# Two tokens per partition for the first four chunks of a retention layer that feeds a gated FFN

## The chip, the cores and the metric

The kernel runs on one core of a Trainium2 chip. A core has TensorE (PE; its weight loads are shown apart as PEld), VectorE (DVE), ScalarE (ACT), GpSimd (POOL) and SyncE (SP), which run their own instruction streams and wait for each other by semaphores. Matmuls read SBUF and write PSUM; DVE and ACT read PSUM; transfers between main memory and SBUF are issued by SP ("hardware" queue), ACT or POOL ("software" queue, which can also convert float32 to bfloat16 on the way). The metric is the device time of one execution in microseconds, the median over several.

## What is computed

Queries, keys and values have shape (4 batches, 8 heads, 768 tokens, 64), all float32. Each head keeps a 64 x 64 state that decays by a factor gamma per token; the result, heads side by side, is a matrix x of 3072 tokens by 512, and goes through a gated FFN of width 1536:

```python
gamma = 1.0 - 2.0 ** (-5.0 - np.arange(H, dtype=np.float32))
for t in range(S):
    state = gamma * state + k[t]^T v[t]
    y[t] = scale * q[t] @ state
gate = 1.0 / (1.0 + np.exp(-(x @ w_gate)))
val = x @ w_val
out = (gate * val) @ w_out
```

## The kernel before

Tokens are cut into chunks of 128 (six to a batch, 24 in all, numbered g) and FFN tiles of 512 tokens (four chunks, six tiles, numbered t). Decay is put into tables: v is scaled by gamma^-s (`scale_v`, L167, table tabv), so that within a batch the state is a plain running sum, and the attention output is scaled by gamma^t (`y_out`, L240, table taby), which also moves it from PSUM to xT, the FFN's input, tokens along the free axis.

For a chunk, q and k are loaded as bfloat16 with tokens on partitions. PE transposes them (four 128 x 128 transposes each; a transpose is a matmul with the identity), ACT copies them to SBUF (qkT). `scores` (L172) makes the 128 x 128 products of keys and queries for eight heads: a head has 64 channels, so a pair of heads takes the upper and the lower half of the array's rows. `masks` (L180) lets DVE multiply them by a causal mask. `inter` (L206) adds q times the state of earlier chunks, which ACT has copied into the block-diagonal tiles zbd (`state_out`, L199); `intra` (L233) adds masked scores times v; `state_early` (L204) adds k^T v to the state in PSUM. Intra and state take half of the array's columns per head.

Two orders matter. The loop from L428 on runs FFN tile after FFN tile (`up`, L278: 4 + 4 matmuls for gate and value of one FFN block n1 of 128 columns, sigmoid on ACT, product on DVE; `down`, L310), with the attention steps of later chunks put between its groups by the table `plan`. Before it, L348 to L410 are a written-out beginning: chunks 0 to 2 go one after another, then `up` of blocks 0 to 3 for the first 384 tokens with chunk 3 in between, and `up_columns` (L292) for the last 128 tokens of these blocks. `keep_on` (L325) issues matmuls of the identity whose result nobody reads. Each engine executes in program order: the schedule is by hand, and only waits are inserted.

The loads are issued in this order. SP: k, q and v of chunk 0 as float32 (kf, qf on L89 to L92, converted on DVE and ACT on L356 and L357; vf). POOL: chunk 1, chunk 2, the first 256 columns of the gate and value weights (`load_gate_val`, L78), chunk 3, the second 256 columns, then the rest, `load_out` (L84) and chunks 4 to 7; two `scale_v` and two extensions of taby stand between them. PSUM has one bank for the state (pool pz) and seven (pool pf, tag ff) that everything else takes in turn, each waiting until the bank's last reader is done.

Of the kernel before, what the change touches and what calls it, by code (L numbers as in the profile page):

```python
# [9 lines left out]
F32 = mybir.dt.float32  # L10
BF16 = mybir.dt.bfloat16
I32 = mybir.dt.int32
AX = mybir.ActivationFunctionType
ALU = mybir.AluOpType
# [3 lines left out]
def kernel(  # L18
# [10 lines left out]
    nc = tc.nc  # L29
# [3 lines left out]
    C = 128  # L33
# [7 lines left out]
    ctx.enter_context(tc.manual_schedule())  # L41
    const = ctx.enter_context(tc.tile_pool(name="const", bufs=1))
    wpool = ctx.enter_context(tc.tile_pool(name="wpool", bufs=1))
    ld = ctx.enter_context(tc.tile_pool(name="ld", bufs=12))
    at = ctx.enter_context(tc.tile_pool(name="at", bufs=2))
    ffn = ctx.enter_context(tc.tile_pool(name="ffn", bufs=3))
    pz = ctx.enter_context(tc.tile_pool(name="pz", bufs=1, space=bass.MemoryType.PSUM))
# [8 lines left out]
    def src(x, g):  # L56
        b, c = divmod(g, NCH)
        return x[b, :, c * C:(c + 1) * C, :].rearrange("h s d -> s h d")

    def load_v(g, eng):  # L60
        vf[g] = ld.tile([C, H, D], F32, tag="vf", name="vf", bufs=8)
        eng.dma_start(out=vf[g], in_=src(v, g))  # L62

    def load_kq(g):
        kn[g] = ld.tile([C, H, D], BF16, tag="kn", name="kn")
# [3 lines left out]

    def load_chunk(g):  # L70
        load_kq(g)
        load_v(g, nc.gpsimd)

    wg = wpool.tile([128, KT, D_FF], BF16, name="wg")
    wv = wpool.tile([128, KT, D_FF], BF16, name="wv")
# [2 lines left out]
    def load_gate_val(s):  # L78
        cols = slice(s * 256, (s + 1) * 256)
        for dst, w in ((wg, moe_w_gate), (wv, moe_w_val)):  # L80
            nc.gpsimd.dma_start(out=dst[:, :, cols],  # L81
                                in_=w.rearrange("(kk p) n -> p kk n", p=128)[:, :, cols])

    def load_out(s):  # L84
# [1 line left out]
                            in_=moe_w_out.rearrange("(n p) d -> p n d", p=128)[:, s * 3:(s + 1) * 3, :])  # L86


    kf = const.tile([C, H, D], F32, name="kf")  # L89
    qf = const.tile([C, H, D], F32, name="qf")  # L90
    nc.sync.dma_start(out=kf, in_=src(k, 0))
    nc.sync.dma_start(out=qf, in_=src(q, 0))  # L92
    nc.scalar.preload_act_table(AX.Exp)
    load_v(0, nc.sync)
    tokv = const.tile([128, NCH], I32, name="tokv")
    nc.gpsimd.iota(tokv, pattern=[[C, NCH]], base=0, channel_multiplier=1)
    ident = const.tile([128, 128], BF16, name="ident")
    make_identity(nc, ident)
    toky = const.tile([128, 384], I32, name="toky")
    nc.gpsimd.iota(toky, pattern=[[1, 384]], base=0, channel_multiplier=0)  # L100
    load_chunk(1)
    causal = const.tile([128, 128], F32, name="causal")
    nc.gpsimd.memset(causal, 1.0)
    nc.gpsimd.affine_select(causal, causal, pattern=[[1, 128]], base=0, channel_multiplier=-1,
                            compare_op=ALU.is_ge, fill=0.0)
    load_chunk(2)

    tabv = const.tile([128, NCH, H], F32, name="tabv")
    for h in range(H):
        nc.scalar.activation(tabv[:, :, h], tokv, AX.Exp, scale=-lg[h])  # L110
    lgp = const.tile([128, NP], F32, name="lgp")
    lsc = const.tile([128, 1], F32, name="lsc")
    nc.vector.memset(lsc, math.log(scale))
# [6 lines left out]
    zbd = [const.tile([128, NP, C], BF16, name=f"zbd{i}") for i in range(4)]  # L120
    for t in zbd:
        nc.vector.memset(t, 0.0)
    taby = const.tile([128, NP, S], F32, name="taby")

    def make_taby(cols):
        for p in range(NP):
            nc.scalar.activation(taby[:, p, cols], toky[:, cols], AX.Exp, scale=lgp[:, p:p + 1], bias=lsc)

    def extend_taby(lo, hi):
        nc.gpsimd.tensor_tensor(taby[:, :, lo:hi], taby[:, :, lo - 384:hi - 384],  # L130
                                gup.unsqueeze(2).to_broadcast([128, NP, hi - lo]), op=ALU.mult)

    causal4 = causal.unsqueeze(1).to_broadcast([128, NP, 128])


# [1 line left out]
    zz, za = {}, {}  # L137

    def bank(shape, dt=F32):
        return pf.tile(shape, dt, tag="ff", name="ff", padded_shape=[128, 2 * NP, C] if dt == BF16 else None)  # L140

    def pair(t, p):
        return t[:, 2 * p:2 * p + 2, :].rearrange("s h d -> s (h d)")

    def transposes(g):
# [3 lines left out]
                nc.tensor.transpose(tp[:, i * NP + p, :], pair(x, p), ident)  # L149
        qkT[g] = at.tile([128, 2 * NP, C], BF16, tag="qkT", name="qkT", bufs=6)  # L150
        nc.scalar.activation(qkT[g], tp, AX.Copy)  # L151

    def transposes_early(g):
        qkT[g] = at.tile([128, 2 * NP, C], BF16, tag="qkT", name="qkT", bufs=6)
        for i, x in enumerate((kn[g], qn[g])):
            tp = bank([128, NP, C], BF16)
            for p in range(NP):
                nc.tensor.transpose(tp[:, p, :], pair(x, p), ident)
            nc.scalar.activation(qkT[g][:, i * NP:(i + 1) * NP], tp, AX.Copy)

    def xbar(g):
        qkT[g] = ld.tile([128, 2 * NP, C], BF16, tag="qkX", name="qkX", bufs=8)
# [4 lines left out]
    def scale_v(g, eng):  # L167
        vs[g] = ld.tile([C, H, D], BF16, tag="vs", name="vs", bufs=8)
        eng.tensor_tensor(vs[g], vf[g], tabv[:, g % NCH, :].unsqueeze(2).to_broadcast([C, H, D]),  # L169
                          op=ALU.mult)  # L170

    def scores(g):  # L172
        t = qkT[g]
        sc[g] = (bank([128, NP, C]), bank([128, NP, C]))
        for p in range(NP):
            for i in range(2):
                half = slice(i * D, (i + 1) * D)
                nc.tensor.matmul(sc[g][i][:, p, :], t[half, p, :], t[half, NP + p, :], start=True, stop=True)  # L178

    def masks(g):  # L180
        stA[g] = at.tile([128, NP, C], BF16, tag="stA", name="stA", bufs=4)
        stB[g] = at.tile([128, NP, C], BF16, tag="stB", name="stB", bufs=4)
        nc.vector.tensor_tensor(stA[g], sc[g][0], causal4, op=ALU.mult)  # L183
        nc.vector.tensor_tensor(stB[g], sc[g][1], causal4, op=ALU.mult)  # L184

    def inter(g):
        y[g] = bank([128, NP, C])
        if g % NCH > 0:
            for p in range(NP):
                nc.tensor.matmul(y[g][:, p, :], zbd[(g - 1) % 4][:, p, :], qkT[g][:, NP + p, :],  # L190
                                 start=(p == 0), stop=False, skip_group_check=True)
# [7 lines left out]
    def state_out(g, z):  # L199
        for i in range(2):  # L200
            half = slice(i * D, (i + 1) * D)
            nc.scalar.copy(zbd[g % 4][half, :, half], z[half])  # L202

    def state_early(g):  # L204
        if g == 0:
            zz[0] = pz.tile([128, 2, NP, D], F32, tag="z", name="z")  # L206
        z = zz[0][:, 0]
        for p in range(NP):
            for i in range(2):
                nc.tensor.matmul(z[i * D:(i + 1) * D, p, :], kn[g][:, 2 * p + i, :], vs[g][:, 2 * p + i, :],  # L210
                                 start=(g == 0 and p == 0), stop=True, skip_group_check=True)
        state_out(g, z)

    def new_za(g):
        za[g] = at.tile([128, NP, D], F32, tag="za", name="za", bufs=3)
        return za[g]
# [16 lines left out]
    def intra(g):  # L233
        first = g % NCH == 0
        for p in range(NP):
            for i, st in enumerate((stA[g], stB[g])):
                nc.tensor.matmul(y[g][i * D:(i + 1) * D, p, :], vs[g][:, 2 * p + i, :], st[:, p, :],  # L237
                                 start=(first and p == 0), stop=True, skip_group_check=True)

    def y_out(g):  # L240
        c = g % NCH
        if g % 4 == 0:
            xT[g // 4] = at.tile([128, NP, 512], BF16, tag="xT", name="xT")
        col = (g % 4) * C
        nc.vector.tensor_tensor(xT[g // 4][:, :, col:col + C], y[g], taby[:, :, c * C:(c + 1) * C], op=ALU.mult)  # L245

    def step_t(g):
        transposes(g)
# [76 lines left out]
    def keep_on(n):  # L325
        u = bank([128, 512])
        for _ in range(n):
            nc.tensor.matmul(u[:, :128], ident, ident, start=True, stop=True)  # L328
# [16 lines left out]
            first += width  # L345


    scale_v(0, nc.gpsimd)  # L348
    load_gate_val(0)
    scale_v(1, nc.gpsimd)  # L350
    load_chunk(3)
    load_gate_val(1)
    make_taby(slice(0, 256))
    kn[0] = ld.tile([C, H, D], BF16, tag="kn", name="kn")
    qn[0] = ld.tile([C, H, D], BF16, tag="qn", name="qn")
    nc.vector.tensor_copy(kn[0], kf)  # L356
    nc.scalar.copy(qn[0], qf)  # L357
    keep_on(30)
    transposes_early(0)
    make_taby(slice(256, 384))  # L360
    extend_taby(384, 512)
    for s in range(2, NFF // 2):
        load_gate_val(s)
    extend_taby(512, 768)
    for s in range(4):
        load_out(s)
    for g in range(4, 8):
        load_chunk(g)
    keep_on(8)
    scores(0)  # L370
    masks(0)
    keep_on(10)
    transposes_early(1)
    inter(0)
    state_early(0)
    intra(0)
    y_out(0)
    keep_on(8)
    scores(1)
    masks(1)  # L380
    keep_on(4)
    inter(1)
    transposes_early(2)
    state_early(1)
    nc.scalar.preload_act_table(AX.Sigmoid)
    intra(1)
    y_out(1)
    scale_v(2, nc.vector)
    keep_on(8)
    scores(2)  # L390
    masks(2)
    inter(2)
    keep_on(14)
    intra(2)
    state_early(2)
    y_out(2)
    up(0, 0, 0, 384)
    scale_v(3, nc.vector)
    transposes_early(3)
    up(0, 1, 0, 384)  # L400
    scores(3)
    masks(3)
    inter(3)
    state_early(3)
    up(0, 2, 0, 384)
    intra(3)
    y_out(3)
    nc.vector.tensor_copy(new_za(3), zz[0][:, 0])
    up(0, 3, 0, 384)
    up_columns(0, range(4), 384, 512)  # L410


    def ups(t):
# [88 lines left out]
```

## Time and profile before

| | us |
|---|---|
| median of 10 executions (233.75 to 237.55) | 234.37 |
| the profiled execution | 234.09 |
| its span, first to last instruction | 232.4 |
| first FFN matmul | 16.74 |
| first FFN matmul on all 512 tokens | 26.01 |
| PE busy | 223.1 (96%) |
| DVE, ACT, POOL busy | 110.8, 91.9, 92.4 |

The profile shows one execution. Its stage table gives busy time per engine; the list of instructions in order of time gives, for a group of like instructions, start, length (from the first's start to the last's end), engine, source line, operation, output and inputs, shape, count, and in brackets the idle time before and what ended it. A matmul's end is modelled, and matmuls are pipelined: those of 128 columns last 0.22 us each and follow each other much closer. `L285` is line 285 of the kernel before; line numbers of the changed kernel differ.

### The profile page before, as it was taken

The numbers are of one execution on the slowest core, as the hardware profiler recorded it, in microseconds if no ns is written. First come the engines' busy times: TensorE is split into PE (matmuls) and PEld (weight loads), VectorE is DVE, ScalarE is ACT, GpSimd is POOL, SyncE is SP. The second block draws the span as 40 slices with busy tenths as digits, with TensorE's granted clock in tenths as the row PEclk, the third lists the DMA queues.
The fourth block names the chain that finished last, engine by engine and source line by source line (L and its number), as shares of the span: only waits on it lengthen the run. The fifth ranks groups of instructions, "written<-read, shape, count | busy, mean of one in ns | idle before, by whom it ended". The sixth has DMA issues, their size and how long they took to land.

```text
span 232.4 us, 4448 instructions
## 1 busy us (share of the span) xinstructions
PE 223.1 (96%) x1781; PEld 125.6 (54%) x1802; DVE 110.8 (48%) x201; ACT 91.9 (40%) x177; POOL 92.4 (40%) x111
## 2 busy tenths in 40 slices
PE   6879999999999999999999999999999999999994
PEld 5655644557889645445445445445445454444444
DVE  5465534175997552374824436717236711243301
ACT  8765333454827332262522432522542422433221
POOL 8999764788798473791164300000000000000000
PEclk9999999999999999999999999999999999999999
DMA  7999999999999999999949752011200012100022
GB/s 139 183 191 168 196 202 201 183 236 226 211 176 151 124 132 185 245 138 134 110 70 206 173 108 53 1 41 52 92 0 3 0 45 75 63 0 0 0 93 90
DMA packets 77556, 27.29 MB, mean 117 GB/s; under 512 B 65056, under 2 KB 73120, under 8 KB 77536
## 3 DMA queue, kind: packets, MB, share of 16 engines
q0 software_dynamic: 57616, 16.78, 73.7%
q1 hardware_dynamic: 19776, 10.16, 21.8%
q8 instruction: 14, 0.23, 0.4%
q10 hardware_dynamic: 144, 0.07, 0.1%
q14 instruction: 6, 0.05, 0.1%
HBM read 28.31 MB, written 6.29 MB: 149 GB/s over the span
## 4 chain that ended last, share of the span: by engine, by line
PE 85%; POOL 6%; DMA 3%; issue 2%; DVE 2%; ACT 1%; POOLq 0%
PE ff L285 46%; PE ff L316 25%; PE ff L299 5%; DMA wv<-in_moe_w_val_dram 3%; PE ff L237 3%; PE ff L178 2%; PE ff L190 2%; PE ff L149 1%; PE ff L336 1%; POOL qn L68 1%; POOL kn L67 1%; POOL vf L62 1%; PE z L196 1%; POOL vs L169 1%; POOL wg L81 1%
## 5 line engine op out<-in xcount | busy, mean ns | idle before, releaser
L290 DVE TENSOR_TENSOR hT<-gs,ff 128x512 bf16<-128x512 f32 (+2 forms) x72 | 45.7, 642 | 68.6 <-PE ff L285 57.0
L285 PE MATMUL ff<-xT,wg 128*128 128x512 bf16 (+2 forms) x277 | 68.0, 361 | 1.3 <-DVE xT L245 0.7
L285 PE MATMUL ff<-xT,wv 128*128 128x512 bf16 (+2 forms) x287 | 68.6, 361 | 0.3 <-DMA wv<-in_moe_w_val_dram 0.2
L289 ACT ACTIVATE gs<-ff 128x512 f32<-128x512 f32 (+2 forms) x72 | 40.4, 562 | 68.2 <-PE ff L285 60.9
L316 PE MATMUL ff<-wo,hT 128*128 128x512 bf16 x267 | 61.1, 379 | 0.9 <-issue 0.5
L285 PEld LDWEIGHTS <-wv 128*128 128x128 bf16 x288 | 28.1, 98 | 29.4 <-DMA wv<-in_moe_w_val_dram 0.6
L316 PEld LDWEIGHTS <-hT 128*128 128x128 bf16 x276 | 26.3, 98 | 31.3 <-DVE hT L290 0.6
L285 PEld LDWEIGHTS <-wg 128*128 128x128 bf16 x288 | 27.1, 98 | 28.3 <-issue 0.7
L321 ACT COPY ob<-ff 128x512 f32<-128x512 f32 x23 | 13.5, 586 | 50.2 <-PE ff L316 38.2
L245 DVE TENSOR_TENSOR xT<-ff,taby 128x512 bf16<-128x512 f32 x24 | 15.6, 687 | 26.0 <-PE ff L237 26.0
L62 POOL DMA_DIRECT2D vf<-in_v_dram x23 | 20.8, 902 | 9.1 <-DVE xT L245 2.9
L169 POOL TENSOR_TENSOR vs<-vf,tabv 128x512 bf16<-128x512 f32 x14 | 14.7, 1054 | 23.1 <-DMA vf<-in_v_dram 19.2
L67 POOL DMA_DIRECT2D kn<-in_k_dram x23 | 20.9, 910 | 2.6 <-DMA wo<-in_moe_w_out_dram 1.1
L68 POOL DMA_DIRECT2D qn<-in_q_dram x23 | 20.4, 889 | 3.5 <-DMA wo<-in_moe_w_out_dram 2.2
L183 DVE TENSOR_TENSOR stA<-ff,causal 128x512 bf16<-128x512 f32 x24 | 16.4, 683 | 2.7 <-PE ff L178 2.6
L184 DVE TENSOR_TENSOR stB<-ff,causal 128x512 bf16<-128x512 f32 x24 | 16.3, 681 | 0.0
L202 ACT CAST zbd<-za 64x256 bf16<-64x256 f32 x32 | 12.9, 403 | 8.6 <-DVE za L224 8.0
L169 DVE TENSOR_TENSOR vs<-vf,tabv 128x512 bf16<-128x512 f32 x10 | 8.0, 804 | 5.4 <-DMA vf<-in_v_dram 5.4
L151 ACT ACTIVATE qkT<-ff 128x1024 bf16<-128x1024 bf16 x8 | 8.2, 1026 | 1.6 <-PE ff L149 1.6
L328 PE MATMUL ff<-ident 128*128 128x128 bf16 x82 | 7.3, 254 | 1.6 <-POOL ident masks.py:199 1.6
L237 PE MATMUL ff<-stB,vs 128*64 128x128 bf16 x96 | 7.9, 222 | 0.4 <-DVE stB L184 0.4
L237 PE MATMUL ff<-stA,vs 128*64 128x128 bf16 x96 | 8.1, 222 | 0.0
(62 smaller groups left out, 141.9 us busy)
## 6 DMA issues: line engine op xcount, KB each, us to landing
vf<-in_v_dram POOLq DMA_DIRECT2D x23, 256.0 KB, 8.3
out_dram<-ob SPq DMA_DIRECT2D x23, 256.0 KB, 3.2
kn<-in_k_dram POOLq DMA_DIRECT2D x23, 128.0 KB, 8.3
qn<-in_q_dram POOLq DMA_DIRECT2D x23, 128.0 KB, 8.3
wg<-in_moe_w_gate_dram POOLq DMA_DIRECT2D x6, 256.0 KB, 7.1
wv<-in_moe_w_val_dram POOLq DMA_DIRECT2D x6, 256.0 KB, 7.6
wo<-in_moe_w_out_dram POOLq DMA_DIRECT2D x4, 384.0 KB, 11.7
kf<-in_k_dram SPq DMA_DIRECT2D x1, 256.0 KB, 3.3
```

The costliest lines, as they stand in the source:

```text
L62: eng.dma_start(out=vf[g], in_=src(v, g))
L67: nc.gpsimd.dma_start(out=kn[g], in_=src(k, g))
L68: nc.gpsimd.dma_start(out=qn[g], in_=src(q, g))
L169: eng.tensor_tensor(vs[g], vf[g], tabv[:, g % NCH, :].unsqueeze(2).to_broadcast([C, H, D]), op=ALU.mult)
L183: nc.vector.tensor_tensor(stA[g], sc[g][0], causal4, op=ALU.mult)
L184: nc.vector.tensor_tensor(stB[g], sc[g][1], causal4, op=ALU.mult)
L237: nc.tensor.matmul(y[g][i * D:(i + 1) * D, p, :], vs[g][:, 2 * p + i, :], st[:, p, :], start=(first and p == 0), stop=True, skip_group_che ...
L245: nc.vector.tensor_tensor(xT[g // 4][:, :, col:col + C], y[g], taby[:, :, c * C:(c + 1) * C], op=ALU.mult)
L285: nc.tensor.matmul(u[:, lo:hi], w[:, kk, n1 * 128:(n1 + 1) * 128], xT[t][:, kk, lo:hi], start=(kk == 0), stop=(kk == KT - 1))
L289: nc.scalar.activation(gs[:, lo:hi], ps[0][:, lo:hi], AX.Sigmoid)
L290: nc.vector.tensor_tensor(hT[t][:, n1, lo:hi], gs[:, lo:hi], ps[1][:, lo:hi], op=ALU.mult)
L316: nc.tensor.matmul(o, hT[t][:, n1, sm * 128:(sm + 1) * 128], wo[:, n1, :], start=(n1 == 0), stop=(n1 == NFF - 1))
```

## The change

The first four chunks are treated as two "runs" of 256 tokens (a = 0, 1). A partition holds two successive tokens, so a row of the load is 512 bytes of float32 where it was 256, and one load brings two chunks. Chunk c of a run lies on partitions 64c to 64c+63, with j = 0, 1 the token within the partition. k and q of both runs, and their conversion, come on POOL's queue; v of both runs on SP's, into the same buffer, so that the second waits for `scale_run(0)`.

Scores, state and intra then contract over 64 rows and write 64 columns or partitions: quarter tiles of the array, 32 matmuls for a run in each of the three, and 16 transposes of 64 output partitions for each of k and q. Masks are taken from a new mask (maskr). The tokens come back into order in `y_out_run`, whose DVE access pattern undoes the interleaving. States of the two chunks are summed on DVE (`sum_run`) before ACT copies them.

`keep_on` goes from 82 matmuls to 24, all at the beginning. The decay tables for v are made by one product on DVE and one exponential on ACT each. taby is split into four tiles. FFN blocks 0 to 3 are computed for tokens 0 to 255 first (`up` of width 256, with chunk 2 and 3's inter and intra between the second and the third), then for tokens 256 to 511 by two `up_columns` of two blocks each. The first gate and value weights are issued after the four loads of q and k; `scale_run(1)` on POOL stands behind the third pair of weight loads. The pool ld has 10 instead of 12 buffers for kn and qn. The order from the fifth FFN block on is unchanged.

```diff
-    kf = const.tile([C, H, D], F32, name="kf")
-    qf = const.tile([C, H, D], F32, name="qf")
-    nc.sync.dma_start(out=kf, in_=src(k, 0))
-    nc.sync.dma_start(out=qf, in_=src(q, 0))
+    vr[0] = load_run(v, 0, F32, nc.sync, "vr")
     nc.scalar.preload_act_table(AX.Exp)
-    load_v(0, nc.sync)
+    kr[0] = load_run(k, 0, BF16, nc.gpsimd, "kr0")
+    ident = const.tile([128, 128], BF16, name="ident")
+    make_identity(nc, ident)
+    tokr = const.tile([128, 2, 2], I32, name="tokr")
+    nc.gpsimd.iota(tokr, pattern=[[2 * C, 2], [1, 2]], base=0, channel_multiplier=2)
...
+    qr[0] = load_run(q, 0, BF16, nc.gpsimd, "qr0")
     toky = const.tile([128, 384], I32, name="toky")
     nc.gpsimd.iota(toky, pattern=[[1, 384]], base=0, channel_multiplier=0)
-    load_chunk(1)
+    kr[1] = load_run(k, 1, BF16, nc.gpsimd, "kr1")
+    qr[1] = load_run(q, 1, BF16, nc.gpsimd, "qr1")
+    maskr = const.tile([128, 2, 2, D], F32, name="maskr")
...
+    load_gate_val(0)
     causal = const.tile([128, 128], F32, name="causal")
...
-    load_chunk(2)
+    load_gate_val(1)
...
+    def load_run(x, a, dtype, eng, name):
+        t = const.tile([128, H, 2 * D], dtype, name=name, tag=name, bufs=1)
+        eng.dma_start(out=t, in_=x[0, :, a * 2 * C:(a + 1) * 2 * C, :].rearrange("h (p j) d -> p h (j d)", j=2))
+        return t
...
+    def transpose_run(x, dst, engines):
+        tp = bank([128, NP, 2, C], BF16)
+        for p in range(NP):
+            for j in range(2):
+                for i in range(2):
+                    nc.tensor.transpose(tp[i * D:(i + 1) * D, p, j, :], runs(x)[:, 2 * p + i, j, :], ident)
...
+    def scores_run(a):
+        for n in range(2):
+            sc[a, n] = (bank([128, 2, 2, C]), bank([128, 2, 2, C]))
...
+                            nc.tensor.matmul(sc[a, n][i][tok, p, j, :], kT[a][half, 2 * n + p, j, tok],
+                                             qT[a][half, 2 * n + p, :, tok], start=True, stop=True)
...
+    def state_run(a):
+        zs = [pz.tile([128, 2, NP, D], F32, tag="z", name="z"), bank([128, 2, NP, D])]
...
+                        nc.tensor.matmul(zs[c][i * D:(i + 1) * D, 0, p, :], runs(kr[a])[tok, 2 * p + i, j, :],
+                                         vsr[a][tok, 2 * p + i, j, :], start=(p == 0 and j == 0), stop=True,
...
+    make_taby(0)
+    scale_run(0, nc.vector)
+    vr[1] = load_run(v, 1, F32, nc.sync, "vr")
+    load_gate_val(2)
+    scale_run(1, nc.gpsimd)
+    extend_taby(3)
+    for s in range(3, NFF // 2):
         load_gate_val(s)
-    extend_taby(512, 768)
+    keep_on(24)
+    kT[0], qT[0], kT[1], qT[1] = (new_run_T() for _ in range(4))
+    transpose_run(kr[0], kT[0], [nc.scalar])
+    state_run(0)
+    state_out(0, zz[0])
+    sum_run(0)
+    sum_run(1)
+    transpose_run(qr[0], qT[0], [nc.scalar, nc.vector])
+    state_out(1, za[1])
+    scores_run(0)
+    masks_run(0, 0)
+    masks_run(0, 1)
+    transpose_run(kr[1], kT[1], [nc.scalar])
+    inter_run(0)
+    inter_run(1)
+    transpose_run(qr[1], qT[1], [nc.scalar])
+    make_taby(2)
+    extend_taby(4)
+    extend_taby(5)
...
     nc.scalar.preload_act_table(AX.Sigmoid)
-    intra(1)
...
+    intra_run(0)
+    y_out_run(0)
+    y_out_run(1)
+    scores_run(1)
+    masks_run(1, 0)
+    state_run(1)
+    sum_run(2)
+    state_out(2, za[2])
+    masks_run(1, 1)
+    sum_run(3)
+    inter_run(2)
+    up(0, 0, 0, 256)
+    up(0, 1, 0, 256)
+    inter_run(3)
+    intra_run(1)
+    y_out_run(2)
+    y_out_run(3)
+    state_out(3, za[3])
+    up(0, 2, 0, 256)
+    up(0, 3, 0, 256)
+    up_columns(0, range(0, 2), 256, 512)
+    up_columns(0, range(2, 4), 256, 512)
```

## The prediction

> **What bounds the kernel now.** I read the page's stage shares first, then busy time by stage, then the order of instructions on each engine up to 27 us, then the waits after 26 us.
>
> ```profile
> span 232.4 us, 4448 instructions
> ...
> PE 223.1 (96%) x1781; PEld 125.6 (54%) x1802; DVE 110.8 (48%) x201; ACT 91.9 (40%) x177; POOL 92.4 (40%) x111
> ```
> ```profile
> 0.00:5.00 5.00, 3.38 (x30) 3.12 (x30) 2.93 (x22) 4.13 (x13) 4.22 (x12) 1.00 0.66 133
> 5.00:16.74 11.74, 9.00 (x156) 7.02 (x157) 6.45 (x10) 8.74 (x18) 11.66 (x15) 1.00 1.74 186
> 16.74:26.01 9.27, 9.06 (x100) 6.02 (x100) 4.95 (x9) 4.33 (x10) 9.27 (x12) 1.00 1.37 178
> 26.01:232.40 206.39, 201.62 (x1498) 109.49 (x1516) 96.51 (x160) 74.74 (x137) 67.21 (x75) 1.00 0.91 110
> ```
> The columns of the stages are the stretch, its length, the busy time of PE, PEld, DVE, ACT and POOL, the granted clock, the DMA share and GB/s. From 26.01 us on PE is the bound, and its waits there are small:
>
> ```profile
> PE ff L316 <- issue: 0.5, 3, 0.2
> PE ff L316 <- DVE hT L290: 0.2, 1, 0.2
> ```
> The code from there on is the same in both kernels, so the end moves with the instant at which PE has finished the first four FFN columns of the first 512 tokens: 26.01 us now. Everything else is the question of how early the changed kernel gets there.
>
> ```profile
> 1.61 3.38 PE L328 MATMUL ff<-ident 128*128 128x128 bf16 x30 [1.61 <-POOL ident masks.py:199]
> ...
> 6.22 0.61 PE L328 MATMUL ff<-ident 128*128 128x128 bf16 x8
> ...
> 12.05 0.40 PE L158 MATMUL ff<-ident,qn 128*128 128x128 bf16 x4 [0.44 <-DMA qn<-in_q_dram]
> ...
> 15.51 0.22 PE L237 MATMUL ff<-stB,vs 128*64 128x128 bf16 x1 [0.38 <-DVE stB L184]
> ...
> 16.74 0.81 PE L285 MATMUL ff<-xT,wg 128*128 128x384 bf16 x4 [0.73 <-DVE xT L245]
> ...
> 21.82 0.82 PE L285 MATMUL ff<-xT,wv 128*128 128x384 bf16 x4 [0.20 <-DMA wv<-in_moe_w_val_dram]
> ...
> 26.01 1.03 PE L285 MATMUL ff<-xT,wg 128*128 128x512 bf16 x3
> ```
> FFN waits until three chunks have gone one after another through load, transpose, scores, mask, intra and scaling. Chunk 2's q lands at 12.05, its last mask at 15.45, its scaled output at 16.69.
>
> **Prices that carry over.** Subtracting the 0.22 us of the last matmul's depth, 128-column matmuls follow each other every 0.106 us in the first group ((3.38-0.31)/29) and every 0.056 us in the second ((0.61-0.22)/7): PE runs at half rate until about 6 us, though the clock column says 1.00. The half-array matmuls go in pairs at the price of one: four pairs of intra matmuls (L237) in 0.22 us, eight state matmuls (L210) in 0.15 us. A DVE instruction of 128x512 takes 0.68 us, 0.60 when another follows; ACT copies 128x512 in 0.60 and 128x1024 in 1.03; POOL's multiply of 128x512 takes 1.07 and that of 128x1024 1.96. POOL spends 0.9 us to issue a chunk load (the first 1.07) and 0.78 a weight load.
>
> **The loads.** Chunk 1's q is waited for until 9.05, chunk 2's until 12.05, with three loads between: 1.0 us of transfer per chunk load. POOL's rows L85 to L67 from 26.68 to 33.24 come 1.3 us apart, each held by the landing of a weight load: 1.33 us for 512 KB read in longer rows. A load of two chunks reads 512 KB in as many pieces as one chunk before, each twice as long. No row has it; it lies between 1.33 (the weight load's bytes in half as many pieces) and 2.0 (two chunk loads), and I take 1.6, near the middle: it shares its bytes with the one and its pieces with the other. Nine one-chunk loads plus three more were 12 us of transfer, six double ones are 9.6.
>
> Then kr0, now POOL's first instruction (0.9 to 1.95), lands at about 5.1 (a chunk load with idle queues takes 3.8 us from issue, plus 0.6 for the double size, within 4.8 to 6.0); qr0 at 6.7, kr1 at 8.3, vr[1] about 10 and qr1 at 11.2. Gate and value blocks 0 follow at 14.3 (12.7 to 16.7 at the ends of the price), blocks 1 at 17 (to 19.4); they are wanted at about 16 and 19. Only at the upper end is this a wait, of 0.7 us at most.
>
> **DVE and ACT up to the first scores.** DVE gains eight memsets for lgh and two small products, which wait for POOL's tokr and tokv at 2.6; the unchanged memsets (0.88 to 3.70 now) then end at 5.6 rather than 3.7. scale_run(0), 128x1024 in one, takes 1.2: v is ready at 6.9. PE has transposed kr0 by 5.9 and waits a microsecond. state_run(0), 32 quarter-tile matmuls: four at the price of one would be 0.25 us, two at a time 0.9; I take 0.5, the rate per instruction that L210 shows. Then ACT's two zbd casts (0.7), DVE's two sums (0.75, held behind ACT), the two halves of the q copy (0.6 each): scores start at 9.0 and DVE is free for masks at 9.7.
>
> **DVE from there on.** Masks of run 0, four of 0.60: to 12.1. Intra and its depth: 0.55 (15.45 to 16.00 in the rows now). Two y_out: 14.0. This is the FFN's input for 256 tokens, against 16.69 for 384 now. Then masks_run(1,0) to 15.2; sum_run(2) (0.4), masks_run(1,1) (1.2) and sum_run(3) (0.4) would end at 17.2.
>
> **POOL.** Its order now carries the other long chain, because scale_run(1) stands behind everything it issues: four loads of q and k (1.07+3x0.9=3.8), ident and iotas (1.2), maskr's fill and two selects (1.8: twice L103's 0.41, then L104's 0.29 raised to 0.5 for twice the columns, two times), six weight loads (4.7), causal (0.7), less 0.3 by which successive rows overlap. From 0.9 that ends at 12.8, and scale_run(1) at 2 us more: 14.8. PE has state_run(1) and inter_run(2) in front of the first FFN matmul, so FFN starts at 14.8 + 0.05 + 0.5 + 0.1 + 0.25 = 15.7, not at 14.0. DVE's sum_run(2) needs the same state at 15.6, 0.4 after it is free, so masks_run(1,1) ends at 17.2 and sum_run(3) at 17.6; a later POOL delays DVE as much.
>
> **PE from FFN's start.** 256-column matmuls come every 0.109 us in the second FFN tile, so each up of 256 is 0.87. up 0 and up 1: 15.7 to 17.5 (up 1 needs the banks that the masks free by 16.6). inter_run(3), intra_run(1) with the 0.1 gap that the rows show when PE goes from whole to half arrays: 18.4. y_out 2 and 3 on DVE: 18.7 to 19.9. up 2 gets its second bank when y_out 2 is done, a wait of 0.5, up 3 to 20.6; two up_columns of 1.75: 24.1. Total PE work is about what it was (7.0 us of FFN on both sides), so the gain is the earlier start less the attention work left after it. I add 0.1 for handovers not counted: 24.2 against 26.0, **-1.8 us**. The removed 52 filler matmuls after the first group were 2.9 us of PE time in waits and count nothing.
>
> Behind that, gate and value blocks 2 to 5 and w_out come 1.33 and 1.9 apart behind blocks 1: w_out's last lands near 36 where 40 is needed, so loading stays ahead. ld's 10 buffers make chunk 14's k wait for chunk 4's state where it waited for chunk 2's; its v already waits for a vf buffer that chunk 6 frees, so nothing new.
>
> The profiled execution took 234.09, 1.7 more than its span and 0.28 less than the median. 234.09-1.8 = 232.3; against the median, 232.6.
>
> [...] The rows show PE reaching full rate at 6.0 after 30 fillers and four transposes, and PE 77% busy from 5.0 to 16.74 thanks to fillers. In the changed kernel it is busy about 5 of the 10 us from 6 to 15.7, longest gap about 1 us. [...]
>
> **Rivals.**
> - *PE stays at half rate into FFN* (slower than before). For it: fillers gone, stretches of 3 us at a third busy. Against it: in the rows it rose with gaps of 0.5. Price: 0.8 on quarter-tile steps, then 16 FFN matmuls at 0.213 for 0.109, 1.7; 2.5 in all, FFN's first columns done at 26.7, 235.1. It decides from 1.8 us on, when the half rate lasts into up 0.
> - *A chain is later but the clock holds*: quarter tiles at two for the price of one (+0.4 in each of state_run 0 and 1 and intra), POOL's new selects or scale_run(1) slowed beside DVE, weight block 0 at its upper bound. Each 0.4 to 0.7; two of them: 233.6.
> - *FFN start follows y_out, not POOL*: POOL half a microsecond quicker changes little, since masks_run(1,1) sets inter_run(3); with double loads at 1.33 and scores earlier by 0.5 those columns are done at 23.4: 231.8.
>
> **Numbers.** Forecast (232.0 to 233.2) 0.50, FFN following y_out (to 231.0) 0.10, later chain (233.2 to 233.9) 0.17, half rate 0.23 with its price anywhere from 1.4 up, of which 0.17 end above 234.8 and 0.06 within 0.2% (0.47 us) of now, about what a measurement of this kernel can tell from no change. The range leaves out half of the better case and the worst of the half-rate case: 231.4 to 235.2. Faster 0.77, same 0.06, slower 0.17.
>
> **What would show it.** Right: kr0's transposes near 5.1; POOL's scale_run(1) ending near 14.8 and the first 256-column FFN matmul near 15.7 after the state matmuls; the first 512-column up near 24.2; and the rest of the span as long as now, 206.4. Wrong: 128-column matmuls 0.106 apart after 6 us, quarter-tile groups longer than 0.5, a DMA wait at the value weights, or FFN waiting on y_out of run 1 beyond 20.

## The result and the profile after

The changed kernel takes 235.47 us (median of 15 executions, 234.69 to 239.49) against 234.22 us for the kernel before (50 executions): 1.0057 times as long, 95% interval 1.0041 to 1.0073. It is slower by about 1.3 us; the forecast was 1.8 us faster. (Ratios here compare only executions in the fast state; medians and ranges take in all.)

The profiled execution took 235.30 us, 1.9 more than its span; before, it was 1.7 more. The page of the kernel after, its first part and the row of the granted clock:

```profile
span 233.4 us, 4591 instructions
...
PE 220.9 (95%) x1851; PEld 125.7 (54%) x1872; DVE 112.0 (48%) x214; ACT 90.8 (39%) x167; POOL 89.7 (38%) x110
...
PEclk9859999999999999999999999999999999999999
```

PE is busy 2.2 us less and the span is 1.0 us longer, so PE now waits, or runs slowly, where it did not. The clock row says where: in the second and third fortieth of the span (5.8 to 17.5 us) it stands at 0.8 and 0.5. The same by stages, cut at the first FFN matmul and at the first one on 512 columns (columns as in the stage table of before):

```profile
5.00:16.64 11.64, 8.90 (x241) 7.25 (x239) 7.59 (x15) 8.39 (x17) 11.26 (x16) 0.71 1.54 203
16.64:26.70 10.06, 8.38 (x103) 6.86 (x101) 6.17 (x13) 5.48 (x11) 9.53 (x13) 1.00 1.45 197
26.70:233.40 206.70, 201.67 (x1497) 109.60 (x1515) 96.77 (x160) 74.80 (x137) 65.09 (x72) 1.00 0.77 107
```

Against the forecast: FFN starts at 16.64 instead of 15.7 (+0.9); from there to the first 512-column matmul it takes 10.06 instead of 8.5 (+1.6); the rest takes 206.70 instead of 206.4 (+0.3). The last 0.2 lies outside the span. Between the first two marks PE's busy time is 8.38 of 10.06 us: it stands for 1.7 us in a stage for which the forecast had a wait of 0.5. The list of PE's instructions in order of time, kernel after:

```profile
6.97 0.64 PE L268 MATMUL ff<-ident,kr 128*64 128x128 bf16 x16 [1.21 <-DMA kr<-in_k_dram]
...
8.41 0.64 PE L268 MATMUL ff<-ident,qr 128*64 128x128 bf16 x16 [0.42 <-DMA qr<-in_q_dram]
...
11.25 1.06 PE L268 MATMUL ff<-ident,kr 128*64 128x128 bf16 x16
...
16.64 0.60 PE L386 MATMUL ff<-xT,wg 128*128 128x256 bf16 x4
...
18.40 0.61 PE L386 MATMUL ff<-xT,wv 128*128 128x256 bf16 x4 [0.29 <-DVE stA L299]
19.18 0.38 PE L308 MATMUL ff<-qkT,zbd 128*128 128x128 bf16 x4 [0.17 <-ACT gs L390]
...
20.07 0.28 PE L386 MATMUL ff<-xT,wg 128*128 128x256 bf16 x1
21.57 0.49 PE L386 MATMUL ff<-xT,wg 128*128 128x256 bf16 x3 [1.22 <-DVE xT L345]
...
26.70 0.38 PE L386 MATMUL ff<-xT,wg 128*128 128x512 bf16 x1
```

Three things are to be seen. The transposes of kr0 start at 6.97, not 5.1. The same 16 transposes take 0.64 us at 7 and 8.4 us and 1.06 at 11.25: the clock was lost in between. And the third FFN block issues one matmul at 20.07 and then stands 1.22 us for DVE's y_out.

That last wait is not in the source. The first matmul of the block reads columns 0 to 255 of row block 0 of xT, the second reads columns 0 to 255 of row block 1. y_out 2 and 3 write columns 256 to 511 of all four row blocks, with the tokens put back in order by a four-dimensional access pattern. In the built program the second matmul waits for y_out 3, which ends at 21.52, though it reads nothing that y_out 3 writes. It looks as if the pattern were taken as one interval, from column 256 of row block 0 to the end of the tile; the test of that is the second run.

### The profile page after: what moved, and what is told of

Read it like the earlier page. It is cut to its first block, busy times and chain, and to the rows that moved or that the text cites. A ratio compares the mean times of both kernels' runs of the same rounds, so it can differ in the third digit from the quotient of the medians.

```text
span 233.4 us, 4591 instructions
## 1 busy us (share of the span) xinstructions
PE 220.9 (95%) x1851; PEld 125.7 (54%) x1872; DVE 112.0 (48%) x214; ACT 90.8 (39%) x167; POOL 89.7 (38%) x110
## 4 chain that ended last, share of the span: by engine, by line
PE 87%; DVE 3%; ACT 3%; issue 3%; DMA 2%; DVEq 0%; POOLq 0%
PE ff L386 45%; PE ff L417 25%; PE ff L400 5%; DMA kr<-in_k_dram 2%; PE ff L247 2%; PE ff L198 2%; PE ff L210 2%; PE ff L177 1%; PE ff L268 1%; PE ff L437 1%; ACT zbd L222 1%; PE z L216 1%; ACT taby L155 1%; ACT L480 1%; DVE stA L203 1%
## 5 line engine op out<-in xcount | busy, mean ns | idle before, releaser
L391 DVE TENSOR_TENSOR hT<-gs,ff 128x512 bf16<-128x512 f32 (+1 forms) x72 | 45.1, 634 | 66.6 <-PE ff L386 61.9
L386 PE MATMUL ff<-xT,wg 128*128 128x512 bf16 (+1 forms) x277 | 67.3, 358 | 1.8 <-DVE xT L345 1.2
L386 PE MATMUL ff<-xT,wv 128*128 128x512 bf16 (+1 forms) x287 | 67.7, 358 | 0.4 <-DVE stA L299 0.3
L390 ACT ACTIVATE gs<-ff 128x512 f32<-128x512 f32 (+1 forms) x72 | 39.8, 556 | 69.6 <-PE ff L386 62.4
L255 DVE TENSOR_TENSOR xT<-ff,taby 128x512 bf16<-128x512 f32 x20 | 12.9, 686 | 23.3 <-PE ff L247 23.3
L203 DVE TENSOR_TENSOR stA<-ff,causal 128x512 bf16<-128x512 f32 x20 | 13.6, 681 | 0.0
L204 DVE TENSOR_TENSOR stB<-ff,causal 128x512 bf16<-128x512 f32 x20 | 13.6, 681 | 0.0
L400 PE MATMUL ff<-xT,wg 128*128 128x256 bf16 x56 | 7.3, 273 | 0.0
L400 PE MATMUL ff<-xT,wv 128*128 128x256 bf16 x56 | 7.3, 273 | 0.0
L406 DVE TENSOR_TENSOR hT<-gs,ff 128x512 bf16<-128x512 f32 x7 | 4.7, 687 | 4.7 <-PE ff L400 3.4
```

The costliest lines, as they stand in the source:

```text
L386: nc.tensor.matmul(u[:, lo:hi], w[:, kk, n1 * 128:(n1 + 1) * 128], xT[t][:, kk, lo:hi], start=(kk == 0), stop=(kk == KT - 1))
L390: nc.scalar.activation(gs[:, lo:hi], ps[0][:, lo:hi], AX.Sigmoid)
L391: nc.vector.tensor_tensor(hT[t][:, n1, lo:hi], gs[:, lo:hi], ps[1][:, lo:hi], op=ALU.mult)
L400: nc.tensor.matmul(u[:, i * n:(i + 1) * n], w[:, kk, n1 * 128:(n1 + 1) * 128], xT[t][:, kk, lo:hi], start=(kk == 0), stop=(kk == KT - 1))
```

## The experiments

The theory after this reading has three parts: a stretch at half clock ahead of the FFN (0.9), the false wait (1.2), and smaller delays on ACT and in the loads. The rival for each: it is a delay beside the path and its removal gives nothing.

**e1_fillers.** Fillers again, in the stretches in which PE waits.

```diff
     sum_run(1)
+    keep_on(9)
     transpose_run(qr[0], qT[0], [nc.scalar, nc.vector])
+    keep_on(16)
```

> The changed kernel with 25 fillers put back: 9 identity matmuls after state_run(0) and 16 after the transposes of run 0's q, where PE waits. Clock theory (the profile's table of stages grants 0.71 of the clock from 5 to 16.6 us because the first stretch was too idle): the clock column stays at 1.00, 128-column matmuls come 0.056 apart from the first scores on, the first FFN matmul starts at 15.8 instead of 16.6 and the first 512-column matmul at about 25.2 instead of 26.7; the time falls by 1.5, to 234.0. Rival theory (loads and DVE set the pace, PE's rate is hidden): the clock may stay up, but the first 512-column matmul stays within 0.3 of 26.7 and the time at 235.5.

The twelve executions spread from 233.42 to 240.66 us, median 236.74. The six below 237 give a ratio to before of 1.0001 (0.9972 to 1.0031), the changed kernel's being 1.0057: about 1.3 us back in these, give or take 0.7. The other six, from 237.41 up, have no part in that ratio. The profiled execution is the longest of all (240.66): v of run 1 landed at 15.19 instead of 13.02, the FFN started at 17.90, and the clock was at half from about 18.0 to 21.4 (256-column matmuls 0.21 us apart there, 0.11 behind it). So no profile of e1 shows what the fillers do in one of its shorter executions.

**e2_halves.** The false wait removed by laying the two halves of the first xT apart, so that no pattern spans both.

```diff
-            xT[0] = at.tile([128, NP, 512], BF16, tag="xT", name="xT")
-        cols = slice(g * C, (g + 1) * C)
+            xT[0] = at.tile([128, 2, NP, 256], BF16, tag="xT", name="xT")
+        cols = slice(g % 2 * C, (g % 2 + 1) * C)
...
-        nc.vector.tensor_tensor(xT[0][:, :, cols].rearrange(in_runs, j=2), y[g].rearrange("x n (j p) -> x n j p", j=2),
+        nc.vector.tensor_tensor(xT[0][:, g // 2, :, cols].rearrange(in_runs, j=2), y[g].rearrange("x n (j p) -> x n j p", j=2),
```

`up` and `up_columns` read the same columns in the new place.

> The changed kernel with the first xT tile laid out as two halves of 256 columns, so that up 2 and up 3, which read the first half, carry no wait for the y_out of run 1, which writes the second. Theory of the added wait (up 2's second matmul stands 1.2 us for a y_out whose columns it does not read): PE runs up 2 and up 3 while DVE does the two y_out, waits 0.3 to 0.4 for a bank in up 2, and the first 512-column matmul comes at 25.7 instead of 26.7; the time falls by 1.0, to 234.5. Rival (the bank of chunk 2's y holds up 2 for as long anyway): 26.5 or later, 235.3.

Median 233.83 us, ratio 0.9974 (0.9958 to 0.9991): faster than both kernels, than the kernel before by 0.6 us. The wait at the third block is gone, so the cause of that wait is shown: the writes of y_out to the other half of the tile, and not a bank. Stages of this run:

```profile
5.00:15.64 10.64, 7.89 (x240) 6.25 (x238) 7.70 (x16) 8.11 (x16) 10.39 (x15) 0.84 1.56 206
15.64:24.64 9.00, 8.26 (x104) 6.80 (x102) 6.03 (x13) 5.79 (x12) 9.00 (x12) 1.00 1.45 197
```

The stage of the first FFN blocks is 1.06 shorter. FFN also starts 1.0 earlier, though nothing ahead of it was edited: in this execution only one stretch of 3.41 us ran at half clock, in the profile of the changed kernel two. So of the 2.3 us between the two profiled executions (235.30 and 233.02) 1.1 is the wait, and 1.0 the clock of these two executions. The one profiled here is the fastest of the twelve; how much of the gain in the medians is clock is not shown.

**e3_both.** Both edits.

> Fillers and halves together. If clock and added wait are the two causes and lie one after the other: first FFN matmul at 15.8, first 512-column matmul at 24.1, 2.6 earlier than in the changed kernel, and 232.9, which is below the kernel before by 1.3. If one hides the other, or a later load or DVE sets the end: between 233.5 and 234.5. If neither counts: 235.5.

Median 233.98, ratio 0.9979 (0.9963 to 0.9994): fillers add nothing to the halves. The gains of e1 and e2 don't add up. This is the middle one of the three expectations: one cause hides the other, or something later sets the end, and which of the two stays open. The profiled execution, the longest of thirteen (236.75), can't tell: v of run 1 landed at 16.21 there, and the FFN started at 18.92.

**e4_before_bare.** The kernel before without its 52 fillers after the first 30, to price what the change took away.

> The kernel before without its 52 later fillers (the first 30 stay). Clock theory: the stretch from about 6 to 9.5 us is then a quarter busy, the clock column falls below 1.00 between about 9.5 and 16.4 us, and the first 512-column FFN matmul comes 0.3 to 1.0 later than 26.0; time 234.5 to 235.2. Rival (the clock falls in the changed kernel for another reason, such as the quarter tiles): clock column 1.00 throughout, time 234.2 or slightly less.

Median 235.65, ratio 1.0053 (1.0030 to 1.0077): 1.2 us slower. PE's list of this run shows what they were for:

```profile
17.50 1.44 PE L285 MATMUL ff<-xT,wg 128*128 128x384 bf16 x4 [0.64 <-DVE xT L245]
18.74 1.48 PE L285 MATMUL ff<-xT,wv 128*128 128x384 bf16 x4
...
23.68 0.82 PE L285 MATMUL ff<-xT,wg 128*128 128x384 bf16 x4
```

The same four matmuls take 1.44 at half rate and 0.82 at full. The granted clock fell at 8.24 and was full again at 21.89, and the first 512-column matmul came at 28.53 instead of 26.01 (in this profiled execution, the longest of its seven). This kernel has no quarter tiles, so they are not needed for the loss. "2.9 us of PE time in waits and count nothing", as the prediction had it, was true of the time and false of the clock.

For the next eight runs the transposes of chunks 12 to 23, which SP's transfers do, were put on PE in all eight alike, far behind the stretch in question; the kernel before stays as it is. They have their own base. A batch of four shares its executions of the kernel before (median 234.29 in the first, 234.78 in the second).

**g0_base.** The changed kernel with those transposes on PE.

> The changed kernel, with one thing else for the tests that follow: q and k of chunks 12 to 23, which SP's transfers transpose, are transposed on PE as chunks 4 to 11 are (96 matmuls, all behind 60 us). Nothing ahead of the fifth FFN block differs, so this is the base for the next runs. PE gets 96 x 0.056 = 5.4 us more work: 240.9 (240 to 242). Theory (a stretch at half clock of about 7 us before the FFN, plus 1.1 to 1.2 us in which PE waits for y_out_run(3)): the granted clock full from about 6, half from about 9.6 to between 13 and 16.5, the first 256-column matmul at 15.6 to 16.7, first 512-column one at 25.7 to 26.7, with the wait of 1.2 us again. Rival (the half rate was an accident of the profiled execution): no half rate after 6 us and the first 512-column matmul near 25.7.

Median 240.47, ratio 1.0255 (1.0196 to 1.0314). The clock column of its profile says 1.00 throughout, yet the 16 transposes at 6.43, 8.00 and 11.12 us all take 1.07: the first record of the clock is at 15.46, and what lies before it counts as full. PE did not lose the full rate here; it had none until 15.46. FFN starts at 17.16, later than either theory had it, because POOL's scale_run(1) waited 1.57 us for v of run 1, which landed at 14.45. That landing varies without any edit to it: nine profiles have this load issued in the same way at 7.3 us (the changed kernel, e1, e2, e3, g0, g2, g3, h1 and h3), and it lands between 12.91 and 16.21. The wait of 1.22 is there again, at 21.44.

**g1_v_held.** v of run 0 is issued only behind POOL's issue of kr0 (one memset on POOL in between).

> The base, with v of run 0 issued only once POOL has issued kr0 (one POOL memset of the buffer's first column behind it). kr0 landed 5.6 us after its issue where 4.4 was forecast. If v's hardware packets hold it off, kr0 lands at 5.3 to 5.8 instead of 6.9, v at 6.3 to 7 instead of 5.1; the score chain gains at most 0.5 of it, because state_run(0) then waits for v: first FFN matmul 0 to 0.5 earlier, time 0 to 0.5 below the base. Rival (a double load simply takes 5.6 us from its issue): kr0 at 6.9 again, v 1.5 later than now, the chain 0.7 to 1 later, 0.5 to 1 above the base.

Median 248.09, 7.6 us above the base. Neither theory had that. kr0 landed a little earlier (its transposes start at 6.14), but this is the chain that ended last, followed back from 30 us:

```profile
2.53 5.43 DMA vr<-in_v_dram
...
9.30 10.25 DMA vr<-in_v_dram
...
19.70 1.91 POOL vsr L278
...
22.84 3.41 PE ff L382 x16
```

v of run 1 shares its buffer with run 0, so its load waits for scale_run(0) and was issued at 9.30 rather than 7.29. It then took 10.25 us instead of 7.17 in the base: 2.0 us later at its issue, 5.1 later at its landing. More of POOL's weight loads are then ahead of it or beside it, but that these are the reason is not shown: in the nine profiles named above the same load took from 5.6 to 8.9 us. All six executions of g1 are long (246.68 to 250.41). PE, idle for 4.4 us until the multiply was done, was at half rate when FFN began (16 matmuls of 256 columns in 3.41 us).

**g2_halves.** The base with the halves apart.

> The base with the halves of the first xT apart, as in the earlier run that did this to the changed kernel. Theory (the wait of the second matmul of the third block is false, and PE stands for it): 1.2 to 1.9 below the base, the first 512-column matmul 1.1 to 2.0 earlier. Rival (the earlier run was faster by its clock, not by the wait): 0 to 0.5 below the base.

Median 239.68, ratio 1.0208 (1.0148 to 1.0268), 0.8 below the base: between the two expectations, with intervals that overlap. The wait of 1.22 is gone, and the first 512-column matmul comes at 25.72 against 26.57. But 0.7 of that is the FFN's start (16.45 against 17.16; v of run 1 landed at 12.98), and from there on this profile takes 9.27 us against 9.41. Of the wait removed, 0.51 comes back as PE's wait for ACT ahead of inter_run(3) and 0.34 as up 1's wait for a bank that the masks of run 1 hold; the base, starting later, had neither.

**g3_taby.** The wait for ACT removed: chunk 2's decay table made on DVE by one product with a new table gup2 of gamma^256, not on ACT by four exponentials ahead of the table load.

```diff
+    nc.vector.tensor_tensor(taby[2], taby[0][:, :, 0:C], gup2.unsqueeze(2).to_broadcast([128, NP, C]), op=ALU.mult)
     state_run(0)
...
-    make_taby(2)
```

> The base with the halves apart, and chunk 2's decay table made on DVE, in its wait of 1.6 us for the casts of run 0, by one product with gamma^256, rather than by four exponentials on ACT. ACT then loads the sigmoid table at about 14.3 instead of 15.9, so the casts of chunk 2's state and the first sigmoids come 0.7 to 1 earlier and PE's wait of 0.60 ahead of inter_run(3) goes. Theory (with the false wait out of the way, ACT's queue is what is late): 0.4 to 0.8 below the halves alone. Rival (masks on DVE set intra_run(1) anyhow): 0 to 0.2 below them.

Median 238.72, ratio 1.0171 (1.0121 to 1.0222), 1.0 below the halves alone, with intervals that overlap. The wait for ACT is gone from its profile, and the first 512-column matmul comes 0.5 earlier, at 25.22.

**h1_fill.** The base with fillers: 34 at the beginning, 9 and 16 as in e1.

> The base (240.4) with filler matmuls again: 34 instead of 24 at the beginning, 9 behind state_run(0), 16 behind the transposes of qr0. Theory (the 128-column matmuls are 0.106 apart up to 14 us or later because PE is too little busy for the clock to rise or to stay): full rate from 6 to 8 us on, the half-array and whole-array groups up to the FFN at half their length, the first 256-column matmul 0.5 to 1.0 earlier, 239.2 to 239.8. Rival (the chain of loads and of POOL sets the FFN's start, and the clock only the steps beside it): the clock rises, and the time stays within 0.3 of 240.4.

**h2_own_vr.** The base with a buffer of its own for v of run 1, loaded on POOL's queue behind qr1, and scale_run(1) ahead of the third pair of weight loads.

```diff
     qr[1] = load_run(q, 1, BF16, nc.gpsimd, "qr1")
+    vr[1] = load_run(v, 1, F32, nc.gpsimd, "vr1")
...
-    vr[1] = load_run(v, 1, F32, nc.sync, "vr")
-    load_gate_val(2)
     scale_run(1, nc.gpsimd)
+    load_gate_val(2)
```

> The base (240.4) with a buffer of its own for v of run 1, loaded on POOL's queue behind qr1 (0.9 of POOL more), and scale_run(1) ahead of the third pair of weight loads (1.5 of POOL earlier). In the base v of run 1 is issued at 7.3, after scale_run(0), and lands 5.7 to 8.9 later depending on the execution; holding v of run 0 back made it 10.3 and cost 7.6 us in all. Theory (a transfer issued on SP behind POOL's queue of loads waits for them, so the shared buffer is the weak point): v of run 1 lands near 12.8 in every execution, scale_run(1) ends at 14.7 to 15.0, the spread of the times shrinks, 239.4 to 240.2. Rival (the landing is not what is late in the usual execution): 240.3 to 240.9, the weight loads 0.9 later.

Medians 240.02 and 241.56, ratios 1.0245 (1.0178 to 1.0312) and 1.0284 (1.0225 to 1.0344): neither can be told from the base. The two profiled executions suggest why. h1, POOL's multiply and the FFN's first matmul:

```profile
14.64 1.90 POOL L276 TENSOR_TENSOR vsr<-vr,tabr 128x1024 bf16<-128x1024 f32 x1 [1.61 <-DMA vr<-in_v_dram]
```
```profile
12.32 0.64 PE L262 MATMUL ff<-ident,qr 128*64 128x128 bf16 x16
...
17.21 0.60 PE L380 MATMUL ff<-xT,wg 128*128 128x256 bf16 x4
```

and h2, the same:

```profile
13.47 1.90 POOL L277 TENSOR_TENSOR vsr<-vr,tabr 128x1024 bf16<-128x1024 f32 x1 [1.52 <-DMA vr<-in_v_dram]
```
```profile
13.09 1.06 PE L263 MATMUL ff<-ident,qr 128*64 128x128 bf16 x16
...
16.85 0.60 PE L381 MATMUL ff<-xT,wg 128*128 128x256 bf16 x4
```

With the clock at full (0.64 for the transposes) v is what is late, and FFN starts at 17.21; with v 1.1 earlier the half clock is (1.06), and FFN starts at 16.85. So in these executions two chains of nearly the same length lead to the FFN's start, PE's own steps and v with POOL's multiply, and each hides what the other's removal would give. The forecast that h2's spread would shrink fell: its executions reach from 240.1 to 243.1.

**h3_no_split.** The base with inter_run(3), intra_run(1) and y_out 2 and 3 ahead of the FFN, whose first four blocks are 512 wide in one.

> The base (240.4) without the changed kernel's last part: inter_run(3), intra_run(1) and y_out 2 and 3 before the FFN, whose first four blocks are then 512 wide in one. The false wait has gone with it. FFN starts when y_out 3 is done, near 21, and four blocks take 4 x 1.73 = 6.9: the first block of the rest at 27.5 to 28, 1 to 1.4 later than in the base, 241.4 to 241.8. So beginning on 256 tokens would be worth about 1 us with its wait. Rival (the clock is what decides, and PE idle before 21 lowers it once more): half rate into the FFN, 242.5 or more. Other rival (the split gains nothing): 240.4.

Median 244.68, ratio 1.0420 (1.0370 to 1.0469), 4.2 above the base: the rival that named the clock. PE's list:

```profile
19.06 0.45 PE L302 MATMUL ff<-qkT,zbd 128*128 128x128 bf16 x4 [2.29 <-ACT zbd L216]
...
22.01 1.86 PE L380 MATMUL ff<-xT,wg 128*128 128x512 bf16 x4 [1.50 <-DVE xT L339]
23.67 1.91 PE L380 MATMUL ff<-xT,wv 128*128 128x512 bf16 x4
...
26.60 1.03 PE L380 MATMUL ff<-xT,wv 128*128 128x512 bf16 x4
```

PE waits 3.8 us for ACT and DVE in these two places. The stretch of 3.41 us up to 19.27 is 33% busy, and from there to about 26.1 PE has half rate (512-column matmuls 0.43 us apart, 0.22 behind it); the 4.1 us of FFN in it cost about 2.0 more than at full rate, an estimate from the two rates. Beginning the FFN on 256 tokens is thus worth about 4 us here: it fills the waits and keeps the clock. No run took another part of the change out by itself, so there is nothing to rank it against.

**h4_best.** All of it: halves, table on DVE, v's own buffer, fillers.

> The base with all of it: halves of xT apart, chunk 2's table on DVE, v of run 1 in its own buffer behind qr1 with scale_run(1) ahead of the third pair of weights, and the fillers. If the causes are separate, their gains add: 238.7 (halves and table) less 0.4 to 1.0 (clock) less 0.2 to 0.8 (v): 237.0 to 238.1. If they are one and the same slack seen from several sides: 238.4 to 238.8.

Median 238.35, ratio 1.0148 (1.0088 to 1.0209), against the base's 1.0255: about 2.5 us, with intervals that overlap a little. That is a bit below the range for one and the same slack and above the range for gains that add. Over g3 (238.72), which has neither fillers nor a buffer of its own for v, it gains 0.4, less than the intervals can tell. Stages of the profiled execution, the fastest of the six (237.27):

```profile
5.00:15.80 10.80, 9.23 (x276) 7.62 (x274) 9.55 (x26) 7.89 (x13) 9.29 (x14) 1.00 1.56 208
15.80:23.68 7.88, 7.88 (x103) 6.95 (x101) 5.37 (x12) 4.23 (x10) 7.88 (x11) 1.00 1.40 185
23.68:235.60 211.92, 208.57 (x1614) 114.93 (x1611) 96.86 (x160) 85.69 (x149) 68.62 (x77) 1.00 0.66 92
```

PE is without a gap from the FFN's start to the first 512-column matmul at 23.68. This version was timed only with the transposes on PE, where it is slower than the kernel before, so the fastest kernel shown is e2's.

## Why the prediction was wrong

*The idea, that all hangs on when the first four FFN columns are done.* Right. The rest of the span is within 0.3 us of the forecast, and h4, with the obstacles gone, does reach the forecast's marks in its fastest execution: FFN at 15.80 (forecast 15.7), 512 columns at 23.68 (24.2).

*"The removed 52 filler matmuls ... count nothing" and the rival of the half rate.* This is the first step that failed. The rival was named, with a price of 2.5 us and 0.23 of the chance; it was set aside because the rows of before showed no loss of clock with gaps of 0.5 us. In the changed kernel it fell at 9.62 all the same. PE's busy time in successive stretches of 3.41 us, kernel after:

```profile
6.20:9.62 3.42, 1.65 (x64) 1.39 (x65) 1.34 (x2) 2.36 (x5) 3.26 (x7) 1.00 1.69 166
9.62:13.03 3.41, 3.00 (x58) 2.26 (x59) 3.20 (x7) 1.79 (x4) 3.33 (x6) 0.50 1.43 263
```

and kernel before:

```profile
6.07:9.48 3.41, 2.56 (x44) 2.02 (x45) 1.29 (x2) 2.96 (x7) 3.41 (x5) 1.00 1.94 180
```

A stretch that is 48% busy (1.65 of 3.42), with no idle time over 0.8 us inside it (waits of 1.21 and 0.93 reach across its ends), was followed by half rate; in e4 1.50 of 3.41 was, and in e2 1.72. Stretches of 2.56 in before, of 2.18 and 2.22 in h1 and h4, of 1.85 in e3 (12.71 to 16.13) and of 1.81 at the end of e4 were not. Nor was the stretch of the kernel after from 19.85 to 23.27, 64% busy (2.20 of 3.42), which has the wait of 1.22 whole inside it. The measurement decides: what fits these runs is the busy share of a stretch, with the limit between 50 and 53%, and not the longest gap in it.

The rival had the mechanism right, but not the place. Full rate is back at 16.44, before the first FFN block, so of its 2.5 us only the part ahead of the FFN was spent. That part was 0.9 (the rival had 0.8): in the six profiles with full clock there (e1, e2, e3, g0, h1 and h4) the FFN starts 0.66 or 0.67 us after scale_run(1) ends, in the changed kernel 1.57. The 1.7 inside the FFN did not come. That the rival's 235.1 and its 26.7 for the first FFN columns lie so near the measured 235.47 and 26.70 is luck; the next step made up the rest.

*"inter3/intra1 ... up 2 gets its second bank when y_out 2 is done, a wait of 0.5".* This is the second step that failed. The wait is not for a bank but for y_out 3, 1.22 long, from a dependence on columns that aren't read. It showed in the order of the built program, where a wait on DVE stood at the second matmul of the block, and not in the diff. It is also one of the prediction's own signs of being wrong: FFN waited on y_out of run 1 until 21.57, beyond 20. A further 0.29 (up 1's value for a bank that the masks of run 1 hold; the sum had it free by 16.6) and 0.17 (ACT's table load ahead of the casts) were not in the sum. Together these waits are 1.7 where 0.5 was forecast; the other 0.4 of the stage's 1.6 is in PE's busy time (8.38, and 7.88 in h4, where PE never waits in this stage). e2 and g2 show that ACT's queue is next when the false wait is gone.

*The loads.* kr0 landed at 6.93, not 5.1. The price of a double load was right: they land 1.47 apart (forecast 1.6, 1.33 to 2.0). The start was wrong: kr0 is issued at 1.32, not 0.9, and takes 5.61 where 4.4 was forecast. (The forecast's own terms, 0.9, 3.8 and 0.6, make 5.3 and not 5.1.) The 3.8 is the price of a load on idle queues (the k load issued at 119.45 in the kernel before); POOL's first chunk load in the kernel before, issued at 1.90 while SP's loads were under way, took 6.1. With v held back (g1) kr0's transposes start at 6.14, against 6.43 to 7.28 in the other runs, so v's load ahead of it may explain a part; the rest stays open. The late landing did not move the FFN by itself: POOL's chain was forecast to be later, and scale_run(1) ended at 15.07 (forecast 14.8).

*The quarter tiles.* Right, at full clock. In e2, 32 state matmuls take 0.45 us from 7.32 (0.5 forecast). The weight loads overlap: in the changed kernel the 32 of this step last 0.11 us each, 3.5 us in sum, and the whole step takes 0.45 from 7.54.

*v of run 1.* The prediction had it landing at about 10, 2.8 us before POOL came to it at 12.8, and left it out of the chain. It landed at 13.02 in the profile of the changed kernel, where POOL came to it at 13.17; in g0 POOL waited for it for 1.6 us. In the two long executions that were profiled (e1 and e3) it landed at 15.19 and 16.21, and the FFN started 1.3 and 2.3 us later than in the changed kernel. A chain that is as long as the one on the path is worth a line even where it is hidden.

## What to carry to other kernels

A filler matmul that hides in a wait has no price in PE time and may still hold the clock (without them e4 ran 13.65 us at half rate): price its removal by counting the busy share of PE that it leaves, not by the longest gap (here, counted over 3.41 us, the clock fell at 50% or less and stayed at 53% or more). Where a tile is written through a strided pattern while others read parts of it, look in the built program for waits between parts that don't overlap, and give the parts their own place in the layout. And when two chains of nearly equal length meet, removing one may show nothing, so remove both in one run too; here that run, h4, has the earlier start in one profile, and no gain over g3 that is clear of the noise.

## What the runs showed of the hardware

- The granted clock changed at steps of 3.41 us or multiples (3.41, 6.83 and, in e4, 13.65 us at half rate). It fell after stretches of 3.41 us that were at most 50% busy (30% in g1, 33% in h3, 36% in e3, 50% in e2) and not after stretches of 53% (the end of e4) or more. It then came back after stretches that were 91% busy or more (91% in g1, 93% in e2, 96% in the changed kernel), and not after stretches of 56 to 88% (56% in h3, 88% in the changed kernel); yet its first rise in the changed kernel came after one of 80% (2.74 of 3.41 us). When it rises at the beginning differs between executions of nearly the same start: 6.20 in the changed kernel, 15.46 in g0, with the same 24 fillers. What decides this is open.
- The clock column counts the time before the first record as full: in g0 it says 1.00 from 5.00 us on, where 16 transposes take 1.07 us and not 0.64. The spacing of 128-column matmuls (0.106 or 0.056 us in the kernel before) tells the truth.
- A 512 KB load on SP's queue took from 5.6 to 8.9 us when issued at 7.3 us in nine profiles, 5.4 when issued at 2.5 and 10.3 when issued at 9.3 (both in g1). What sets this spread is open.
- The changed kernel and most of its variants take 1.9 us more than their spans; the kernel before, e4, g3, h3 and h4 take 1.7. Nothing here tells why.
